# One PSUM pool for a whole attention and feed-forward kernel, with a new prologue order and a new load order

## The chip, the cores and the metric

One core of one Trainium2 chip. The metric is the device time of one execution in microseconds (us), as a median over several runs; the reading is done on a profile of one execution, whose span runs from the first to the last instruction of the program. "PE" is the matrix engine, "PEld" its weight loads, "DVE" VectorE, "ACT" ScalarE, "POOL" GpSimd. PSUM is the memory that PE writes its results to, in banks; a drain is the copy or product with which ScalarE or VectorE empties a bank, and a pair is two banks used as one tile.

## The reference

Eight heads, batch 4, 768 rows of 64. An 8x8 matrix per head is made doubly stochastic by five rounds of exp and normalising, and mixes the eight blocks of 96 rows of keys and of values. Each block of queries then attends to its mixed block. The result, 3072 x 512, goes through a gated feed-forward layer.

```python
k_sorted = einsum('bhij,bhjcd->bhicd', P, k_b); v_sorted = einsum(..., P, v_b)
attn = softmax(scale * q_b @ k_sorted^T);  x = (attn @ v_sorted) -> [B*S, H*D]
g = x @ w_gate;  out = (silu(g) * (x @ w_val)) @ w_out
```

## The kernel before

Work is cut into half batches. Feed-forward block n (there are eight, 0 to 7) takes the x of half batch n: 12 gate and 12 value groups of four matmuls, and output groups of the block before. Attention and mixing of later batches are strewn between them as side work. A "unit" is two heads by four blocks: scores, exp, value product, division, transpose to x. The first half of batch 0 has nothing to hide beside and is the prologue. All loads go through one queue in the order of issue.

```python
wide = tc.tile_pool(name="wide", bufs=1, space=PSUM); psum = wide.__enter__()   # prologue's pool
...
for m in range(0, DF, 256):                 # six pairs of pieces of the gate and value weights
    load_gv(m, m + 256)
load_k(1, 0, C); load_q(1, 0, C); load_v(1, 0, C)      # batch 1
nc.gpsimd.dma_start(out=wo_sb, in_=wo_dram)
...
for n in range(4):                          # batch 0: values and keys in turn
    v_wide(n, "s", slots[2 * n % 3])        # "s": drained by ScalarE
    kq_wide(n, "v", slots[(2 * n + 1) % 3]) # "v": drained by VectorE
...                                         # four units, whole, then:
wide.__exit__(None, None, None)
psum = ctx.enter_context(tc.tile_pool(name="psum", bufs=3, space=PSUM))  # main part
# tags: "att" 3 banks (scores, mixing, x), "av" one pair (value products), "gen" 3 banks
...
def units(b, us):                           # side work, with costs
    ... qk(b, us[n]) / av(b, us[n-1]) / xtr(b, us[n-2], "v")
merge(ffn(0), units(0, range(4, 8)) + kqs(1))
merge(ffn(1), [v_chunk(1, ...) x8] + units(1, range(4)))
```

The softmax here doesn't subtract the row's maximum and nothing guards it: scores larger than these inputs give would overflow.

Of the kernel before, what the change touches and what calls it, by code (L numbers as in the profile page):

```python
# [17 lines left out]
def kernel(  # L18
# [46 lines left out]
    wide = tc.tile_pool(name="wide", bufs=1, space=bass.MemoryType.PSUM)  # L65
    psum = wide.__enter__()
# [67 lines left out]
    for m in range(0, DF, 256):  # L134
        load_gv(m, m + 256)
    load_k(1, 0, C)
    load_q(1, 0, C)
    load_v(1, 0, C)
# [31 lines left out]
    def pair_tile(name, slot):  # L170
        return psum.tile([128, 1024], FP32, name=name, tag=slot)

    def bank_tile(name, slot):
        return psum.tile([128, 512], FP32, name=name, tag=slot)

    p_ps = pair_tile("p_ps", "wa")[0:BH, 0:NB * NB].rearrange("p (i j) -> p i j", j=NB)
# [40 lines left out]
    def kq_chunk(b, cb, eng, tag):  # L217
        nat = kq_tiles[b]
        dst = kqt_tile(b).rearrange("p (n c) -> p n c", c=C)
        rm = rmix[b].rearrange("p two a g i -> p two (a g i)")  # L220
        tp = psum.tile([128, 8, 2 * GI], FP32, name="tkq", tag=tag)
        for lc in range(8):
            for two in range(2):
                nc.tensor.matmul(tp[two * D:(two + 1) * D, lc, :],  # L224
                                 lhsT=nat[:, cb * 8 + lc, :],
                                 rhs=rm[:, two, :], start=True, stop=True)
        drain(eng, dst[:, :, ts(cb, 8)], tp.transpose([0, 2, 1]))

    def v_chunk(b, db, eng, tag):
        rows = highr if b % 2 else lowr  # L230
        dst = vt_tile(b // 2)[:, b % 2]
        mix = vmix[b // 2][rows, b % 2].rearrange("p a b -> p (a b)")
        tp = psum.tile([128, 8, H * NB], FP32, name="tv", tag=tag)
        for ld in range(8):
            at = (db * 8 + ld) * C
            nc.tensor.matmul(tp[:, ld, :], lhsT=vch[rows, at:at + 128], rhs=mix,  # L236
                             start=True, stop=True)
        drain(eng, dst[:, :, ts(db, 8)], tp[0:C].transpose([0, 2, 1]))

    def v_pair_chunk(pair, db, eng, tag):  # L240
        dst = vt_tile(pair).rearrange("p u n e -> p (u n) e")
        mix = vmix[pair].rearrange("p u a b -> p (u a b)")
        tp = psum.tile([128, 4, 2 * H * NB], FP32, name="tv", tag=tag)
        for ld in range(4):
            at = (db * 4 + ld) * C
            nc.tensor.matmul(tp[:, ld, :], lhsT=vch[:, at:at + 128], rhs=mix,  # L246
                             start=True, stop=True)
        drain(eng, dst[:, :, ts(db, 4)], tp[0:C].transpose([0, 2, 1]))
# [4 lines left out]
    def qk(b, u):  # L253
        half, g = divmod(u, H2)
        flat = kqts[b]
        pss = [psum.tile([128, 4, C], FP32, name=f"qk{two}", tag="att") for two in range(2)]
        for i4 in range(4):
            at = (g * NB + half * 4 + i4) * C
            for two in range(2):
                lo = two * D  # L260
                nc.tensor.matmul(pss[two][:, i4, :], lhsT=flat[lo:lo + D, at:at + 128],  # L261
                                 rhs=flat[lo:lo + D, GI * C + at:GI * C + at + C],
                                 start=True, stop=True)
        mine = []
        for two in range(2):
            e = e_all[:, ecount[0] % 8, :]
            ecount[0] += 1
            nc.scalar.activation(e[:, 0:4 * C], pss[two][0:C].rearrange("p a c -> p (a c)"),  # L268
                                 AF.Exp, scale=scale)
            mine.append(e)  # L270
        es[(b, u)] = mine

    def av(b, u, tag="av"):
        half, g = divmod(u, H2)
        vt = vts[b // 2][:, b % 2].rearrange("p (h i) e -> p h i e", h=H)
        av_ps = psum.tile([128, 2, 512], FP32, name="av_ps", tag=tag, bufs=1)
# [14 lines left out]
    def xtr(b, u, eng, tag="att"):  # L291
# [3 lines left out]
        st = sts.pop((b, u))  # L295
        x_ps = psum.tile([128, 4, C], BF16, name="x_ps", tag=tag, bufs=1 if tag == "we" else 3)
        for i4 in range(4):
            nc.tensor.transpose(x_ps[:, i4, :], st[:, i4].rearrange("p a b -> p (a b)"),  # L298
                                ident[0:C, 0:C])
        drain(eng, xts[(b, half)][:, g, :], x_ps.rearrange("p a b -> p (a b)"))  # L300
# [5 lines left out]
    def gate(n, m):  # L306
        xt = xts[divmod(n, 2)]
        if m == 0:
            h_tiles[n] = hpool.tile([128, NFC, TW], BF16, name=f"h{n}", tag="h")
        g_ps = psum.tile([128, TW], FP32, name="g_ps", tag="gen")  # L310
        for kc in range(NKC):
            nc.tensor.matmul(g_ps, lhsT=wg_sb[:, kc, ts(m, 128)], rhs=xt[:, kc, :],  # L312
                             start=(kc == 0), stop=(kc == NKC - 1))
        th_sb = gsp.tile([128, TW], BF16, name="th_sb", tag="th")
# [6 lines left out]
    def value(n, m):  # L321
        xt = xts[divmod(n, 2)]
        v_ps = psum.tile([128, TW], FP32, name="v_ps", tag="gen")
        for kc in range(NKC):
            nc.tensor.matmul(v_ps, lhsT=wv_sb[:, kc, ts(m, 128)], rhs=xt[:, kc, :],  # L325
                             start=(kc == 0), stop=(kc == NKC - 1))
        nc.vector.scalar_tensor_tensor(h_tiles[n][:, m, :], v_ps, 0.5, gs_tiles.pop(m),  # L327
# [4 lines left out]
    def outp(n, t3, part):  # L332
        b, half = divmod(n, 2)
        h_w = h_tiles[n]
        if part == 0:
            o_tiles[n] = psum.tile([128, DM], FP32, name="o_ps", tag="gen")
# [11 lines left out]
    idle_ps = bank_tile("idle_ps", "wd")  # L348

    def fill(n, width=512):  # L350
        for _ in range(n):
            nc.tensor.matmul(idle_ps[:, 0:width], lhsT=warm_sb[:, 0:128], rhs=warm_sb[:, 0:width],
                             start=True, stop=True)

    for _ in range(84):
# [3 lines left out]
                     rhs=v_tiles[0][lowr, HC:HC + 2, :].rearrange("p c d -> p (c d)"),  # L359
                     start=True, stop=True)  # L360
    fill(9)

    w_ps = bank_tile("w_ps", "we").rearrange("p (s i b h) -> p s i b h", s=2, b=B, h=H)

    def weights(half):
        for i in range(NB):
            nc.tensor.matmul(w_ps[half * R:(half + 1) * R, half, i].rearrange("p b h -> p (b h)"),
# [6 lines left out]
    def mix_of(b):  # L374
# [5 lines left out]
            w_ps[lo:lo + R, b % 2, :, b].transpose([0, 2, 1]), op=ALU.mult)  # L380
# [3 lines left out]
            w_ps[0:R, 0, :, b].rearrange("p i (g two) -> p two g i", two=2), op=ALU.mult)  # L384

    def qk_wide(u):
        half, g = divmod(u, H2)
        flat = kqts[0]
        ps = pair_tile("qk", ["wa", "wb", "wc", "wc"][u]).rearrange("p (two n) -> p two n", two=2)
        for i4 in range(4):  # L390
            at = (g * NB + half * 4 + i4) * C
            for two in range(2):
                lo = two * D
                nc.tensor.matmul(ps[:, two, i4 * C:(i4 + 1) * C], lhsT=flat[lo:lo + D, at:at + 128],
                                 rhs=flat[lo:lo + D, GI * C + at:GI * C + at + C],
                                 start=True, stop=True)
        n = ecount[0] % 8
        ecount[0] += 2
        nc.scalar.activation(e_all[:, n:n + 2, 0:4 * C], ps[0:C, :, 0:4 * C], AF.Exp, scale=scale)  # L399
        es[(0, u)] = [e_all[:, n, :], e_all[:, n + 1, :]]  # L400

    mix_of(0)
    kdst = kqt_tile(0).rearrange("p (n c) -> p n c", c=C)
    rm = rmix[0].rearrange("p two a g i -> p two (a g i)")

    def kq_wide(cb, engs, slot):
        tp = pair_tile("tkq", slot).rearrange("p (l n) -> p l n", n=2 * GI)
        for lc in range(16):
            for two in range(2):
                nc.tensor.matmul(tp[two * D:(two + 1) * D, lc, :],  # L410
                                 lhsT=kq_tiles[0][:, cb * 16 + lc, :],
                                 rhs=rm[:, two, :], start=True, stop=True)
        w = 16 // len(engs)
        for n, eng in enumerate(engs):
            drain(eng, kdst[:, :, cb * 16 + n * w:cb * 16 + (n + 1) * w],
                  tp[:, n * w:(n + 1) * w].transpose([0, 2, 1]))

    vdst = vt_tile(0)[:, 0]
    vm = vmix[0][lowr, 0].rearrange("p a b -> p (a b)")

    def v_wide(db, eng, slot):
        tp = pair_tile("tv", slot).rearrange("p (l n) -> p l n", n=H * NB)
        for ld in range(16):
            at = (db * 16 + ld) * C
            nc.tensor.matmul(tp[:, ld, :], lhsT=vch[lowr, at:at + 128], rhs=vm,
                             start=True, stop=True)
        drain(eng, vdst[:, :, ts(db, 16)], tp[0:C].transpose([0, 2, 1]))

    for b in range(1, B):
        mix_of(b)  # L430
    slots = ["wa", "wb", "wc"]
    for n in range(4):
        v_wide(n, "s", slots[2 * n % 3])
        kq_wide(n, "v", slots[(2 * n + 1) % 3])
    kq_wide(4, "s", slots[8 % 3])
    kq_wide(5, "sv", slots[9 % 3])
    fill(3)
    qk_wide(0)
    qk_wide(1)
    qk_wide(2)  # L440
    av(0, 0, "wa")
    av(0, 1, "wb")
    xtr(0, 0, "s", "we")
    av(0, 2, "wa")
    qk_wide(3)
    fill(1)
    xtr(0, 1, "s", "we")
    av(0, 3, "wb")
    fill(1)
    xtr(0, 2, "s", "we")  # L450
    fill(2)
    xtr(0, 3, "s", "we")
    fill(2)
# [3 lines left out]
    wide.__exit__(None, None, None)  # L457
# [102 lines left out]
```

## Time and profile before

| | before |
|---|---|
| time, median of 3 timed runs | 274.19 us (273.6 to 274.84) |
| profiled execution: span, its own time | 273.3 us, 275.36 us |
| PE busy share | 93% |

A block's length is the difference of two starts, that of the first gate matmuls (the prediction lists them).

### The profile page before, as it was taken

Reading aid. Unit: us, or ns where it says so; the run is one execution under the profiler, and the core shown is the slowest. Engines: PE = TensorE matmul, PEld = TensorE weight load, DVE = VectorE, ACT = ScalarE, POOL = GpSimd, SP = SyncE. Lnnn points to the kernel's source line nnn. Section 1 sums busy time; section 2 is a strip of 40 time slices with the busy share of each in tenths; the row PEclk is TensorE's granted clock in tenths of the full one; section 3 lists DMA queues with packets and bytes.
Section 4 is the critical chain, followed back from the end, with each engine's and each line's share of the span. In section 5 each row is a group of like instructions: output and inputs, shape, how many; then the busy total and the mean of one; then the engine's idle time right before and its main releaser. Section 6 shows DMA issues by size and latency. Waiting matters only on the chain.

```text
span 273.3 us, 6511 instructions
## 1 busy us (share of the span) xinstructions
PE 254.0 (93%) x2775; PEld 147.0 (54%) x2775; DVE 163.8 (60%) x362; ACT 125.9 (46%) x242; POOL 47.2 (17%) x46
## 2 busy tenths in 40 slices
PE   3786984999998999999999999999999999999994
PEld 3374452665555556556655556555555555555541
DVE  6685493675369488456359487466566766566500
ACT  3876631446752534439963435335332534323311
POOL 7766300793029300000000000000000000000000
PEclk9998898899999999999999999999999999999998
DMA  6979999909996101101101101101110111011122
GB/s 114 209 98 171 197 224 200 183 4 193 210 232 138 41 1 41 41 2 38 41 0 42 38 0 41 41 4 38 41 38 2 38 38 41 1 41 38 40 77 77
DMA packets 12700, 20.86 MB, mean 76 GB/s; under 512 B 896, under 2 KB 8576, under 8 KB 12032
## 3 DMA queue, kind: packets, MB, share of 16 engines
q0 software_dynamic: 9168, 14.16, 29.4%
q1 hardware_dynamic: 3504, 6.30, 6.2%
q8 instruction: 21, 0.34, 0.5%
q14 instruction: 7, 0.06, 0.1%
HBM read 28.32 MB, written 6.29 MB: 127 GB/s over the span
## 4 chain that ended last, share of the span: by engine, by line
PE 78%; DMA 13%; DVE 3%; POOL 3%; issue 1%; ACT 1%; ACTq 0%; POOLq 0%
PE o_ps L339 23%; PE v_ps L325 22%; PE g_ps L312 21%; DMA kq<-in_q_dram 6%; PE tkq L224 4%; DMA kq<-in_k_dram 4%; DMA wv_sb<-in_moe_w_val_dram 3%; PE qk L261 2%; PE av_ps L281 2%; PE x_ps L298 1%; PE tv L246 1%; PE tv L236 1%; DVE h L327 1%; DVE gs_sb L317 1%; POOL wg_sb L101 1%
## 5 line engine op out<-in xcount | busy, mean ns | idle before, releaser
L317 DVE SCALAR_TENSOR_TENSOR gs_sb<-th_sb,g_ps 128x384 bf16<-128x384 bf16 x96 | 53.0, 552 | 64.0 <-ACT th_sb L315 62.4
L312 PE MATMUL g_ps<-xt,wg_sb 128*128 128x384 bf16 x384 | 78.9, 328 | 0.1
L325 PE MATMUL v_ps<-xt,wv_sb 128*128 128x384 bf16 x384 | 78.9, 328 | 0.0
L315 ACT ACTIVATE th_sb<-g_ps 128x384 bf16<-128x384 f32 x96 | 47.5, 495 | 58.2 <-PE g_ps L312 57.3
L339 PE MATMUL o_ps<-wo_sb,h 128*128 128x512 bf16 x288 | 68.6, 379 | 0.0
L327 DVE SCALAR_TENSOR_TENSOR h<-v_ps,gs_sb 128x384 bf16<-128x384 f32 x96 | 53.3, 555 | 7.8 <-PE v_ps L325 0.6
L312 PEld LDWEIGHTS <-wg_sb 128*128 128x128 bf16 x384 | 34.7, 98 | 22.8 <-issue 1.4
L325 PEld LDWEIGHTS <-wv_sb 128*128 128x128 bf16 x384 | 34.0, 98 | 20.3 <-issue 0.3
L339 PEld LDWEIGHTS <-h 128*128 128x128 bf16 x288 | 26.5, 98 | 27.5
L344 ACT COPY o_sb<-o_ps 128x512 f32<-128x512 f32 x24 | 14.1, 587 | 54.4 <-PE o_ps L339 54.3
L114 POOL COPY vch<-v 64x1536 bf16<-64x1536 bf16 (+1 forms) x10 | 28.0, 2856 | 33.4 <-DMA v<-in_v_dram 33.4
L268 ACT ACTIVATE e_all<-qk 96x384 bf16<-96x384 f32 x56 | 24.3, 488 | 5.7 <-PE qk L261 5.6
L206 ACT CAST vt<-tv 96x512 bf16<-96x512 f32 (+1 forms) x28 | 21.8, 808 | 6.5 <-PE tv L236 3.4
L204 DVE CAST kqt<-tkq 128x512 bf16<-128x512 f32 (+1 forms) x23 | 17.9, 778 | 8.2 <-PE tkq L224 6.4
L287 DVE TENSOR_TENSOR st<-av_ps,r_sb 96x512 bf16<-96x512 f32 x32 | 21.9, 684 | 0.7
L206 ACT CAST kqt<-tkq 128x512 bf16<-128x512 f32 (+1 forms) x20 | 12.1, 604 | 11.4 <-PE tkq L224 10.7
L224 PE MATMUL tkq<-rmix,kq 128*64 128x64 bf16 x576 | 12.9, 200 | 3.6 <-DMA kq<-in_q_dram 3.6
L224 PEld LDWEIGHTS <-kq 128*64 128x64 bf16 x576 | 10.9, 115 | 9.8 <-issue 9.8
L281 PEld LDWEIGHTS <-e_all 96*128 96x128 bf16 x256 | 12.0, 99 | 7.5 <-ACT e_all L399 1.7
L281 PE MATMUL av_ps<-vt,e_all 96*128 96x65 bf16 x256 | 13.7, 195 | 2.0 <-ACT e_all L399 1.2
L298 PEld LDWEIGHTS <-st 96*128 96x128 bf16 x128 | 8.9, 100 | 8.1 <-DVE st L287 3.7
L298 PE MATMUL x_ps<-ident,st 96*128 96x96 bf16 x128 | 11.2, 211 | 2.1 <-DVE st L287 2.1
(59 smaller groups left out, 121.8 us busy)
## 6 DMA issues: line engine op xcount, KB each, us to landing
out_dram<-o_sb SPq DMA_DIRECT2D x24, 256.0 KB, 2.0
kq<-in_q_dram POOLq DMA_DIRECT2D x4, 768.0 KB, 13.2
kq<-in_k_dram POOLq DMA_DIRECT2D x3, 768.0 KB, 13.1
v<-in_v_dram POOLq DMA_DIRECT2D x3, 768.0 KB, 17.7
wg_sb<-in_moe_w_gate_dram POOLq DMA_DIRECT2D x6, 256.0 KB, 9.5
wv_sb<-in_moe_w_val_dram POOLq DMA_DIRECT2D x6, 256.0 KB, 10.0
wo_sb<-in_moe_w_out_dram POOLq DMA_DIRECT2D x1, 1536.0 KB, 24.2
v<-in_v_dram POOLq DMA_DIRECT2D x2, 384.0 KB, 5.6
```

Of the source, the lines that this page charges most:

```text
L114: eng.tensor_copy(dst, src.transpose([0, 2, 1]))
L206: nc.scalar.copy(dst, src)
L224: nc.tensor.matmul(tp[two * D:(two + 1) * D, lc, :], lhsT=nat[:, cb * 8 + lc, :], rhs=rm[:, two, :], start=True, stop=True)
L268: nc.scalar.activation(e[:, 0:4 * C], pss[two][0:C].rearrange("p a c -> p (a c)"), AF.Exp, scale=scale)
L281: nc.tensor.matmul(o[:, two, i4, :], lhsT=e[:, i4 * C:i4 * C + 128], rhs=vt[:, 2 * g + two, half * 4 + i4, :], start=True, stop=True)
L298: nc.tensor.transpose(x_ps[:, i4, :], st[:, i4].rearrange("p a b -> p (a b)"), ident[0:C, 0:C])
L312: nc.tensor.matmul(g_ps, lhsT=wg_sb[:, kc, ts(m, 128)], rhs=xt[:, kc, :], start=(kc == 0), stop=(kc == NKC - 1))
L315: nc.scalar.activation(th_sb, g_ps, AF.Tanh, scale=0.5)
L317: nc.vector.scalar_tensor_tensor(gs_sb, th_sb, 1.0, g_ps, op0=ALU.add, op1=ALU.mult)
L325: nc.tensor.matmul(v_ps, lhsT=wv_sb[:, kc, ts(m, 128)], rhs=xt[:, kc, :], start=(kc == 0), stop=(kc == NKC - 1))
L327: nc.vector.scalar_tensor_tensor(h_tiles[n][:, m, :], v_ps, 0.5, gs_tiles.pop(m), op0=ALU.mult, op1=ALU.mult)
L339: nc.tensor.matmul(o_ps, lhsT=h_w[:, m, ts(t3, 128)], rhs=wo_sb[:, m, :], start=(m == 0), stop=(m == NFC - 1))
```

## The change

Its intent: keep one PSUM pool from start to end (pairs "a" and "b", one bank "x", three banks "gen"), so that no pool is swapped; share the drains of the prologue between two engines and mix all values of batch 0 before the keys; load batch 1's keys and queries before the last pair of weight pieces; place side work by fractions of a block; start the first gate and value matmuls on those head pairs whose x is there.

```diff
-    wide = tc.tile_pool(name="wide", bufs=1, space=bass.MemoryType.PSUM)
-    psum = wide.__enter__()
+    psum = ctx.enter_context(tc.tile_pool(name="psum", bufs=1, space=bass.MemoryType.PSUM))
-    for m in range(0, DF, 256):
+    for m in range(0, 1280, 256):
         load_gv(m, m + 256)
     load_k(1, 0, C)
     load_q(1, 0, C)
+    load_gv(1280, DF)
...
-    def qk(b, u):                            # two single banks, two exps
+    def qk(b, u, tag="b"):                   # one pair, one exp over both
-    def av(b, u, tag="av"):
+    def av(b, u, tag="a"):
...                                           # x of the main part: tag "att" -> the one bank "x"
+    v_chunk(0, 0, 8, "v", "gen"); v_chunk(0, 8, 16, "s", "a"); ...   # all values
+    kq_chunk(0, 0, 16, "v", "a"); kq_chunk(0, 16, 16, "s", "b"); ... # then keys
...
+    early(0, (0,)); early(1, (0,))           # first gate and value on head pair 0
+    x3 = ...                                 # x of the fourth unit
+    early(0, (1, 2)); early(1, (1, 2)); early(2, (0, 1, 2))
+    for n in range(3): early(n, (3,))
...
-    merge(ffn(1), [v_chunk x8] + units(1, range(4)))
+    merge(ffn(1), spread([v_chunk x4 of double size], 0.4, 0.6) + spread(units(1, range(4)), 0.6, 0.97))
-    merge(ffn(2), units(1, range(4, 8)) + kqs(2))
+    merge(ffn(2), spread(units(1, range(4, 8)), 0.0, 0.45) + spread(kqs(2), 0.45, 0.95))
```

(Cut: more warm-up fillers, the copy of the mixing weights to SBUF, the same spreading of the later blocks.)

## The prediction

> **What bounds the kernel now.** I read the page first for the busiest engine, then the chain that ended last, then the chain and the waits inside the first 60 us, then a table by stage.
>
> ```profile
> PE 254.0 (93%) x2775; PEld 147.0 (54%) x2775; DVE 163.8 (60%) x362; ACT 125.9 (46%) x242; POOL 47.2 (17%) x46
> PEclk9998898899999999999999999999999999999998
> PE 78%; DMA 13%; DVE 3%; POOL 3%; issue 1%; ACT 1%; ACTq 0%; POOLq 0%
> ```
>
> The matrix engine carries the chain for 78%, but 13% of it is DMA. The chain between 10 and 52 us shows where that part lies:
>
> ```profile
> 4.98 10.80 DMA kq<-in_k_dram
> ...
> 19.67 9.42 DMA wv_sb<-in_moe_w_val_dram
> 29.09 0.29 issue
> 29.38 15.68 DMA kq<-in_q_dram
> 45.06 0.14 issue
> 45.19 0.69 PE tkq L224 x32
> 45.89 1.00 PE v_ps L325 x4
> 46.89 1.28 PE g_ps L312 x4
> ```
>
> Until 45.19 us nothing that PE does is on the chain. Batch 0's keys land, then the weights (twelve pieces), then batch 1's keys and queries, and only then can PE mix batch 1. The waits of PE from 29.6 to 52 us, and the stages, say what it costs (columns of the table: stretch, length, busy time of PE, PEld, DVE, ACT and POOL, clock, DMA share, GB/s):
>
> ```profile
> PE tkq L224 <- DMA kq<-in_q_dram: 3.6, 1, 3.6
> 12.20:21.80 9.60, 7.72 (x278) 6.49 (x278) 7.04 (x13) 6.03 (x7) 5.97 (x9) 1.00 0.81 114
> 21.80:29.64 7.84, 6.13 (x87) 3.77 (x87) 3.74 (x11) 4.82 (x8) 3.91 (x7) 0.78 1.43 189
> 29.64:41.50 11.86, 10.80 (x124) 6.41 (x124) 9.37 (x22) 5.67 (x13) 1.84 (x3) 1.00 1.27 216
> 41.50:50.00 8.50, 4.94 (x77) 2.94 (x77) 3.06 (x6) 2.15 (x4) 0.60 (x1) 0.80 1.07 197
> 59.45:90.54 31.09, 30.38 (x278) 16.62 (x277) 18.16 (x38) 15.11 (x31) 14.78 (x11) 1.00 0.79 170
> 90.54:121.79 31.25, 31.18 (x405) 18.14 (x404) 21.26 (x42) 13.97 (x29) 0.66 (x1) 1.00 0.08 27
> ```
>
> The cuts are the starts of the feed-forward blocks (48 gate matmuls each): 29.64, 59.45, 90.54, 121.79, 152.92, 184.17, 210.97, 237.77. From 59 us on PE is full, and a block there only gets shorter by matmuls or switches that vanish. The loose time is before 59 us: 9.6 us of mixing for batch 0, 7.8 us for its first four attention units, and 8.5 us with a 3.6 us wait and a clock of 0.80.
>
> **What the Trainium skill says.** "TensorE: Matmul & The Clock Gate", Part 1, has PE drop to half clock after about one idle window of 3.4 us. The trace agrees: after the 3.6 us wait, the clock record shows 0.5 from 46.26 for 3.41 us, and four matmuls take 1.00 and 1.28 us against 0.65 elsewhere. "DMA: Bandwidth & Descriptors", Queues, rings and completion order: each DMA engine consumes its descriptors in ring order. Here the pool's loads landed in the order of issue, so moving one load moves those behind it by its length. "VectorE: DVE Perf Modes", Why PSUM operands drop a tier: an fp32 PSUM source runs at 1x. The trace agrees: 0.69 us for 128x512 and 1.22 for 128x1024, so one drain in place of two saves only 0.16. "PSUM — Partial Sum Buffer", Specifications: eight banks of 2 KiB per partition. Both pools fill them: before, 3+3+2 in the main part; after, two pairs (a, b), one bank for x and three "gen" banks.
>
> **The change part by part.**
>
> *Load order.* The sixth pair of weight pieces goes behind batch 1's keys and queries. In the trace the tenth weight piece landed at 34.45, the eleventh and twelfth at 35.76 and 37.6, keys at 41.22, queries at 45.06. Keys then take 3.62 us and queries 3.84, so without the pair the queries land at 34.45+3.62+3.84 = 41.9. That is 3.15 us earlier. The late pair lands near 44.9 and is first wanted by the gate of chunk 10, three matmul groups after batch 1's mixing begins, near 46. Values of batch 1 (49.3) and the output weights (56.2) keep their times, since the same bytes precede them.
>
> *Batch 0's mixing.* Now it starts at 13.09 and the last drain ends at 21.73. VectorE works 5.01 us on four wide key drains, 0.69 on the last, and 1.3 on mixes of batches 1 to 3 in between. ScalarE has four value drains of 1.06, one of 1.01 and one of 0.59. After, the drains are shared: VectorE 0.67+1.2+0.67 for values and 1.22+0.69+1.22+0.69 for keys, 6.4 us; ScalarE 1.06+0.6+0.6 and 1.01+0.59+0.59+1.01, 5.5 us, plus a 0.4 us copy of the weights. The mixes of the other batches read that copy and stand behind the drains, where VectorE waited 1.77 us anyway. The filler and warm-up in front end before the softmax does (11.5), so weights start at about 11.7, not 12.21, values at 12.55. 12.95 + 6.4 + about 0.6 of hand-overs gives the first score matmul at T = 20.0, where it is 21.79.
>
> *First four units.* Counted from T with before's durations (exp 0.81 for a pair or 2 x 0.49, reciprocal 0.20, multiply 0.69): the four results are ready at 2.6, 3.5, 4.7, 5.8. Two units' x leave in one ScalarE copy (estimate 0.8, ends 5.2), the third at 5.7, the fourth by VectorE at 6.5. Nine of the twelve first gate and value matmuls run on the pairs present, and only three wait for the last: all twelve end at T+7.7 = 27.7. Before, the first gate starts at 29.64, T+7.85, and three groups need 1.96 us more, to 31.6. The price: the three groups hold all three "gen" banks, so the next value waits until ScalarE's tanh (0.49) and VectorE's product (0.55) free one, about T+8.6 = 28.6. Net 3.0 us ahead.
>
> *Block 0.* Fourteen groups of 0.652 and the four units of the second half (3.2 us of PE: 0.37 score, 0.265 value, 0.17 transpose each) come before batch 1's mixing: 28.6+9.1+3.2 = 40.9. VectorE must do 14 products of 0.55, 0.35 of copies and four units of 1.23, 12.9 us in the 12.3, so PE is held about 0.5 more: 41.4. The queries come at 41.9. The 3.56 us wait shrinks to some 0.5 us, and the half-clock stretch (3.4 us of work took 5.0, 1.6 lost) should vanish. The rest is 7 groups and six chunks of 0.72: 4.6+4.3 = 8.9, plus 0.3 for drains of 1.22 at tight spacing. Block 1 starts at 51.2, where it is 59.45: 8.2 us. Of these, about 3 are the prologue, 1.6 the clock, the rest the wait.
>
> *Later blocks.* The matmul counts are unchanged (768 mixing, 192 value mixing, 256+256+128 attention, 768+288 feed-forward). The eight half-row value chunks of batch 1 become four; each run costs about 0.19 more for its switches (first matmul to step 0.258 where 0.163 is usual, last 0.122 against 0.03), 0.75 saved. The spread by fractions puts two whole groups between the last unit's value matmul and its transpose, where 0.9 us was lost at 86 us and 0.6+0.3 near 148: I count 0.5 and 0.7 back. Blocks 2 and 4 gain 0.15 each; 5, 6 and the tail are as before.
>
> Sum: 51.2 + 29.8 + 31.1 + 30.4 + 31.1 + 26.8 + 26.8 + 35.6 = 262.8 of span. The timed median is 0.9 above the profiled span (274.19 against 273.3): 263.7. I add 0.6 for waits I have not seen: 264.3.
>
> **Rivals.** *The next transfer takes over.* With block 1 at 51.2 the output weights (56.2) are wanted at 51.2+8 x 0.652 = 56.4, and batch 1's values, rearranged by POOL until about 60.6, at about 61.0. For: neither transfer moves. Against: both are met by a few tenths. If the margins fail it costs 0.5 to 2 us: 265 to 266. *VectorE becomes the bound of block 0.* It has 22.4 us of work for PE's 21.2 there. For: 9.37 busy of 11.86 already. Against: the second stretch, with drains split, is lighter. It would add 1 to 2 us: 265 to 266. *The clock falls in the prologue.* It was 0.78 in the second stretch. For: PE waits for exp and multiply there as before; a 3.4 us window at half clock under the twelve matmuls costs up to 1.7 us. Against: seven fillers of 0.22 fill the gaps. 265.5. *All is hidden:* if the queries still landed at 45, only the clock and the later blocks would gain, 270; the ring order speaks against it.
>
> **Range and chances.** The three costly rivals together reach 268, and nothing found makes it slower; the best case without the 0.6 and with the whole of the lost waits back is 262. So 264.3, 262.0 to 267.8. Two per cent is 268.7: faster 0.93, within 0.06, slower 0.01.
>
> **What would show it.** Right: batch 1's queries landing at about 42 and a wait under 1 us there, no half clock after it, first score matmul near 20.0, block 1 starting near 51. Wrong: the queries landing after 44, a new wait of more than 1 us on the output weights or on the rearranged values, a gap of more than 1.5 us on the "gen" banks after the first twelve matmuls, or blocks 1 to 4 longer than before.

## The result, and the profile after

The changed kernel took 270.81 us (269.81 to 271.1, four runs) against 274.19. Ratio 0.987, 95% interval 0.9834 to 0.9905; a ratio is the mean time of one kernel's fast runs over that of the other's fast runs of the same rounds, so not quite the ratio of the medians. It is faster by 1.3%, where 3.6% was forecast. It lies outside the range, and within the two per cent to which the prediction gave a chance of 0.06.

The page of the changed kernel, first busy times and the clock:

```profile
span 267.7 us, 6445 instructions
PE 250.7 (94%) x2756; PEld 146.5 (55%) x2781; DVE 169.9 (63%) x362; ACT 114.9 (43%) x189; POOL 47.3 (18%) x46
PEclk9999999999999999999999999999999999999999
PE 82%; DVE 9%; ACT 5%; issue 3%; ACTq 0%; DVEq 0%
```

The clock is full in all slices, and DMA has gone from the chain that ended last (it was 13%). In its place stand VectorE with 9% and ScalarE with 5%: the chain now passes through drains and exps. The stages by block follow, cut at block starts (columns as in the prediction: stretch, length, busy times of PE, PEld, DVE, ACT and POOL, clock, DMA share, GB/s). Before, blocks 3 and 4:

```profile
121.79:152.92 31.13, 30.54 (x278) 18.50 (x277) 17.36 (x36) 20.92 (x39) 0.00 (x0) 1.00 0.07 27
152.92:184.17 31.25, 31.18 (x405) 18.14 (x404) 21.27 (x42) 13.97 (x29) 0.00 (x0) 1.00 0.07 27
```

After, the prologue's mixing and units, and blocks 0 to 4 (the first row of the fence is the prologue):

```profile
12.20:25.28 13.08, 11.77 (x344) 8.92 (x347) 10.67 (x23) 9.57 (x16) 7.94 (x12) 1.00 0.94 134
25.28:51.92 26.64, 24.34 (x375) 14.75 (x373) 21.11 (x43) 11.68 (x20) 7.59 (x8) 1.00 1.23 207
51.92:81.73 29.81, 29.52 (x274) 16.80 (x276) 20.14 (x39) 12.58 (x21) 13.48 (x11) 1.00 0.81 169
81.73:113.98 32.25, 31.10 (x402) 18.18 (x404) 20.36 (x39) 13.53 (x22) 8.29 (x3) 1.00 0.17 46
113.98:146.22 32.24, 30.52 (x275) 18.72 (x277) 21.55 (x40) 15.16 (x23) 0.00 (x0) 1.00 0.07 25
146.22:178.47 32.25, 31.10 (x402) 18.18 (x404) 20.35 (x39) 13.53 (x22) 0.00 (x0) 1.00 0.07 26
```

Blocks 2, 3 and 4 have the same matmuls as before, and in blocks 2 and 4 the same PE busy time within 0.1 us, yet each is 1.0 to 1.1 us longer than before: PE has gaps there. The two kernels' accounts, in us:

| | before | after | change | forecast |
|---|---|---|---|---|
| start of block 1 | 59.45 | 51.92 | -7.53 | 51.2 |
| block 1 | 31.09 | 29.81 | -1.28 | 29.8 |
| block 2 | 31.25 | 32.25 | +1.00 | 31.1 |
| block 3 | 31.13 | 32.24 | +1.11 | 30.4 |
| block 4 | 31.25 | 32.25 | +1.00 | 31.1 |
| blocks 5 and 6 | 53.6 | 53.3 | -0.3 | 53.6 |
| rest | 35.5 | 35.9 | +0.4 | 35.6 |
| span | 273.3 | 267.7 | -5.6 | 262.8 |

The waits of PE between 80 and 180 us name the gaps (columns: engine and line, what it waited for, us in total, times, longest). Before:

```profile
PE x_ps L298 <- DVE st L287: 1.2, 2, 0.7
```

After:

```profile
PE x_ps L304 <- DVE xt L204: 2.1, 3, 0.8
PE g_ps L323 <- DVE h L346: 0.8, 1, 0.8
PE qk L267 <- ACT e_all L276: 0.7, 3, 0.2
```

All three are new. Before, a transpose waited for its own input (st, the divided result). Now it waits for xt, the copy that empties the bank of the transpose before it. A gate waits for h, the product that empties a "gen" bank. And scores wait for an exp, that is for the pair "b" to be read. The timeline of the changed kernel at one such place (start, length, engine, line, operation, and in brackets the idle time and its releaser; lines of other instructions left out where dots stand):

```profile
93.89 0.35 PEld L304 LDWEIGHTS <-st 96*128 96x128 bf16 x4
94.05 0.34 PE L304 MATMUL x_ps<-ident,st 96*128 96x96 bf16 x4
...
94.22 0.82 PE L323 MATMUL g_ps<-xt,wg_sb 128*128 128x384 bf16 x4
94.34 0.68 DVE L293 TENSOR_TENSOR st<-av_ps,r_sb 96x512 bf16<-96x512 f32 x1
94.94 0.54 DVE L346 SCALAR_TENSOR_TENSOR h<-v_ps,gs_sb 128x384 bf16<-128x384 f32 x1
...
95.40 0.34 DVE L204 COPY xt<-x_ps 128x384 bf16<-128x384 bf16 x1
95.80 0.33 PE L304 MATMUL x_ps<-ident,st 96*128 96x96 bf16 x4 [0.76 <-DVE xt L204]
```

The third unit's transpose is done at 94.39. Its copy has to queue behind the fourth unit's multiply (94.34) and a product (94.94), and starts at 95.40. The fourth transpose had its input from 95.02 on, but there is one bank "x", so PE stands until 95.80. Before, x took its bank from the three of the tag "att". Between the two transposes stands one gate group (94.22).

The listing counts idle time from the modelled ends of matmuls. By their starts PE lost more: from the last gate matmul to the transpose it is 1.08 us, where 0.16 is the usual step, so 0.92. The losses of single waits named below (0.92, 0.71, 0.94, 0.31, 0.28, 0.89) are by starts.

### The profile page after: what moved, and what is told of

It is laid out like the page before. It is cut to its first block, busy times and chain, and to the rows that moved or that the text cites. A ratio compares the mean times of both kernels' runs of the same rounds, so it can differ in the third digit from the quotient of the medians.

```text
span 267.7 us, 6445 instructions
## 1 busy us (share of the span) xinstructions
PE 250.7 (94%) x2756; PEld 146.5 (55%) x2781; DVE 169.9 (63%) x362; ACT 114.9 (43%) x189; POOL 47.3 (18%) x46
## 3 DMA queue, kind: packets, MB, share of 16 engines
q0 software_dynamic: 9168, 14.16, 29.8%
## 4 chain that ended last, share of the span: by engine, by line
PE 82%; DVE 9%; ACT 5%; issue 3%; ACTq 0%; DVEq 0%
PE o_ps L358 23%; PE v_ps L341 21%; PE g_ps L323 21%; PE tkq L226 6%; PE qk L267 3%; PE av_ps L287 2%; PE x_ps L304 2%; DVE h L346 2%; ACT e_all L276 2%; PE tv L238 2%; DVE gs_sb L333 2%; ACT th_sb L331 1%; DVE st L293 1%; PE tv L248 1%; DVE vt L204 1%
## 5 line engine op out<-in xcount | busy, mean ns | idle before, releaser
L341 PE MATMUL v_ps<-xt,wv_sb 128*128 128x384 bf16 x380 | 77.6, 326 | 0.8 <-DVE gs_sb L333 0.8
L323 PE MATMUL g_ps<-xt,wg_sb 128*128 128x384 bf16 x376 | 76.6, 326 | 0.8 <-DVE h L346 0.8
L331 ACT ACTIVATE th_sb<-g_ps 128x384 bf16<-128x384 f32 x96 | 46.9, 490 | 67.8 <-PE g_ps L323 65.2
L358 PE MATMUL o_ps<-wo_sb,h 128*128 128x512 bf16 x268 | 67.3, 380 | 1.3 <-DVE h L346 0.2
L276 ACT ACTIVATE e_all<-qk 96x768 bf16<-96x768 f32 x30 | 24.0, 802 | 13.5 <-PE qk L267 13.3
L291 DVE RECIPROCAL r_sb<-av_ps 96x8 f32<-96x8 f32 x32 | 6.4, 200 | 19.3 <-PE av_ps L287 19.2
L226 PEld LDWEIGHTS <-kq 128*64 128x64 bf16 x768 | 14.1, 112 | 7.1 <-issue 7.0
L204 DVE CAST kqt<-tkq 128x1024 bf16<-128x1024 f32 (+1 forms) x13 | 14.8, 1138 | 4.5 <-PE tkq L226 4.5
L226 PE MATMUL tkq<-rmix,kq 128*64 128x64 bf16 x768 | 16.6, 197 | 0.8 <-issue 0.8
L206 ACT CAST kqt<-tkq 128x1024 bf16<-128x1024 f32 (+1 forms) x13 | 12.1, 948 | 8.4 <-PE tkq L226 8.3
```

Source lines behind the costliest of these rows:

```text
L226: nc.tensor.matmul(tp[two * D:(two + 1) * D, lc, :], lhsT=kq_tiles[b][:, at + lc, :], rhs=rm[:, two, :], start=True, stop=True)
L276: nc.scalar.activation(e_all[:, n:n + 2, 0:4 * C], wide[0:C, :, 0:4 * C], AF.Exp, scale=scale)
L323: nc.tensor.matmul(g_ps, lhsT=wg_sb[:, kc, ts(m, 128)], rhs=xt[:, kc, :], start=(kc == 0), stop=(kc == NKC - 1))
L331: nc.scalar.activation(th_sb, g_ps, AF.Tanh, scale=0.5)
L341: nc.tensor.matmul(v_ps, lhsT=wv_sb[:, kc, ts(m, 128)], rhs=xt[:, kc, :], start=(kc == 0), stop=(kc == NKC - 1))
L358: nc.tensor.matmul(o_ps, lhsT=h_w[:, m, ts(t3, 128)], rhs=wo_sb[:, m, :], start=(m == 0), stop=(m == NFC - 1))
```

## The experiments

Nine kernels start from the changed one (the control is the changed kernel itself), three from the kernel before. All twelve gave the right result. Ratios are against the kernel before, run on the same chip in the same rounds; three chips were used, one for each group of four.

| run | median us | ratio (95% interval) | span | block 1 starts | blocks 1, 2, 3, 4 |
|---|---|---|---|---|---|
| after_again | 270.55 | 0.9863 (0.982 to 0.9906) | 267.3 | 51.54 | 29.82, 32.25, 32.23, 32.25 |
| load_only | 276.0 | 1.0056 (1.0018 to 1.0094) | 272.9 | 57.05 | 33.07, 31.25, 31.12, 31.26 |
| old_load | 272.51 | 0.9921 (0.9888 to 0.9954) | 271.6 | 55.82 | 29.81, 32.25, 32.23, 32.26 |
| no_early | 269.77 | 0.9825 (0.9796 to 0.9853) | 267.0 | 51.28 | 29.81, 32.25, 32.23, 32.25 |
| x_scalar | 267.65 | 0.9759 (0.9716 to 0.9801) | 267.8 | 54.55 | 29.72, 31.59, 31.53, 31.59 |
| x_gen | 269.89 | 0.9833 (0.981 to 0.9857) | 268.6 | 53.27 | 29.77, 31.89, 31.53, 31.89 |
| qk_swap | 268.66 | 0.9796 (0.9772 to 0.982) | 266.6 | 51.75 | 29.82, 31.94, 31.93, 31.94 |
| combo | 265.89 | 0.9696 (0.9655 to 0.9738) | 263.3 | 51.89 | 29.73, 31.28, 30.28, 31.28 |
| load_warm | 276.2 | 1.0019 (0.9981 to 1.0058) | 273.8 | 55.01 | 36.01, 31.26, 31.12, 31.26 |
| load_warm_vlate | 272.94 | 0.9927 (0.9895 to 0.9958) | 269.8 | 55.65 | 30.97, 31.26, 31.12, 31.26 |
| old_banks | 267.38 | 0.9709 (0.9679 to 0.9739) | 265.3 | 53.53 | 30.25, 31.23, 30.21, 31.23 |
| combo_whole | 264.81 | 0.9647 (0.9604 to 0.969) | 261.9 | 50.5 | 29.72, 31.28, 30.28, 31.28 |

A profile is of one run, and the first 60 us vary: after, x_scalar, x_gen, qk_swap and combo differ before block 1 only in the four units of block 0, and block 1 starts anywhere from 51.75 to 54.55. Blocks 2 to 4 repeat within 0.02 us in the two profiles of the changed kernel. So the blocks are compared by the profile and the whole by the ratio.

### Control: after_again

No edit.

> Control: the changed kernel once more on the chip of the other three runs. Both theories: 270 to 271.5, span 267.5 to 269, blocks 2, 3 and 4 about 32.2 each. It also tells how far one profiled span lies below or above the timed median (the prediction took 0.9; the records of both kernels suggest about 2).

It came as expected, with six runs from 269.42 to 272.84. The profiled run's own time is 269.42, 2.1 above its span of 267.3. In the first pair of profiles it is the same: 275.36 against 273.3 and 269.81 against 267.7.

### What the load order does: old_load, load_only

old_load: the changed kernel, weights first again.

```diff
-    for m in range(0, 1280, 256):
+    for m in range(0, DF, 256):
         load_gv(m, m + 256)
     load_k(1, 0, C)
     load_q(1, 0, C)
-    load_gv(1280, DF)
```

> The changed kernel with all weights ahead of batch 1's keys, as before. My theory: queries land near 44.6, where PE asks for them at 42.6, so 2 us more than the changed kernel, 272.5 to 273, and perhaps a short half clock on top. Rival (the later place of batch 1's mixing already covers the load): within 0.5 us of the changed kernel.

Median 272.51, as expected: 0.6% more than the changed kernel on the same chip. The queries landed at 45.62 and PE waited for them (waits of PE from 26 to 70 us, old_load):

```profile
PE tkq L225 <- DMA kq<-in_q_dram: 2.9, 1, 2.9
```

After it the clock record shows half speed from 45.29 for 3.41 us, and block 1 starts at 55.82 instead of 51.54. So the load order is a real part of the gain, about 2 us by the medians (the two intervals overlap a little, but the wait is in the trace), and the new prologue does not cover the late load. The profiled run is the slowest of its six, at 273.72, so the 4.3 us at block 1 overstate it.

load_only: the kernel before with the load order of the changed one.

```diff
-    for m in range(0, DF, 256):
+    for m in range(0, 1280, 256):
         load_gv(m, m + 256)
     load_k(1, 0, C)
     load_q(1, 0, C)
+    load_gv(1280, DF)
```

> The kernel before with the new load order alone. My theory (the wait for batch 1's queries and the half clock after it cost 5.2 us in the kernel before, and the blocks 2 to 4 of the changed kernel give 3 us of the gain back): queries land near 41.9, the 3.6 us wait falls under 0.7, no half clock after it, 4 to 5 us faster than before, so as fast as the whole change or up to 1 us faster (269 to 270.5). Rival (the wait was hidden by VectorE's backlog and comes back elsewhere): under 2 us faster, 272 or more.

This was a miss: 276.0 us, 0.6% slower than before, where I had expected 4 to 5 us less. The queries did land at 41.88, the wait for them is gone, and block 0 takes 24.82 us instead of 29.81, 5.0 less, as my theory said. The stages of load_only show where it went (prologue mixing, prologue units, block 0, block 1):

```profile
12.20:23.72 11.52, 10.09 (x278) 8.69 (x277) 7.07 (x13) 6.23 (x7) 7.23 (x11) 0.70 0.84 122
23.72:32.23 8.51, 7.31 (x86) 4.41 (x87) 3.83 (x11) 4.93 (x8) 3.94 (x7) 0.62 1.45 196
32.23:57.05 24.82, 23.77 (x368) 14.66 (x369) 19.16 (x40) 11.92 (x26) 8.47 (x4) 0.99 1.04 186
57.05:90.12 33.07, 30.44 (x278) 16.62 (x276) 18.15 (x38) 15.12 (x31) 17.60 (x12) 1.00 0.75 160
```

In the prologue PE ran at a clock of 0.70 and 0.62, so block 0 began at 32.23, 2.6 us later than in the profile of before. In the kernel before such a delay is hidden, because PE waits for the queries until 45 us anyway. Its runs on that chip agree: the five with a mean clock of 0.978 to 0.981 have a mean span of 272.6, the five with 0.993 or 0.994 one of 272.7. And block 1 is 2.0 us longer: its first value chunk waits for the values of batch 1, which POOL rearranges until about 60 us. 5.0 - 2.6 - 2.0 leaves 0.4, the difference of the two spans (273.3 and 272.9). This is the account of one pair of profiles: load_only's is the fastest of its six runs, before's a slow one. By the medians load_only is 1.2 us slower, not 0.4 faster, and these 1.6 us are not accounted for.

### The two things that ate it: load_warm, load_warm_vlate

load_warm: load_only with the changed kernel's warm-up.

```diff
-    for _ in range(84):
+    for _ in range(82):
-                     rhs=v_tiles[0][lowr, HC:HC + 2, :]
+                     rhs=v_tiles[0][lowr, 0:2, :]
-    fill(9)
+    fill(11)
```

> load_only with the changed kernel's warm-up in front (82 small matmuls, the first half of the values as marker, eleven fillers). Theory: load_only lost in the prologue what it won at the queries, because PE ran at half clock from 15.5 to 22.4 and 25.8 to 32.6 us and block 0 began at 32.2, and nothing hid it any more. With PE warm from about 11 us on, block 0 begins at 29.7 or before, and the time falls 2 to 3.5 us against load_only (273 to 274). Rival (the half clock comes from the idle times of the prologue itself, not from its start): half clock stays in the record and the time stays at 275 to 276.

The expected gain did not come; the time is 276.2. The half clock did not go: it stands in the record from 15.54 for 6.83 us, though not from 25.8 to 32.6 as in load_only, and block 0 starts at 30.34. So the warm-up in front is not what keeps PE at full clock. What PE saved there it lost at once in a longer wait (waits of PE from 26 to 70 us, and a piece of the chain that ended last: start, length, what):

```profile
PE tv L237 <- POOL vch L114: 3.3, 1, 3.3
```

```profile
30.25 18.18 DMA v<-in_v_dram
...
51.38 8.38 POOL vch L114 x3
59.75 0.05 issue
59.80 0.54 PE tv L237 x8
60.34 1.40 PE g_ps L313 x4
```

The next transfer, batch 1's values with their rearrangement on POOL, has taken the place of the queries. It ends at 59.8, and at 60.5 in load_only, where block 1 began 2 us later; and the matmuls behind it run at half clock again (1.40 us for four). The prediction had this rival, but for the changed kernel, whose value chunks come later; the kernel before asks for them first thing in block 1.

load_warm_vlate: the same, with the value chunks of batch 1 moved behind the first output group of block 1.

```diff
-    merge(ffn(1), [(0.28, lambda db=db: v_chunk(1, db, "s", "att")) for db in range(8)]
+    merge(ffn(1), [(1.5, lambda: None)] + [(0.28, lambda db=db: v_chunk(1, db, "s", "att")) for db in range(8)]
           + units(1, range(4)))
```

> load_warm with the value chunks of batch 1 put after the first output group of block 1. Theory: in load_only they waited 2.0 us for the values that POOL rearranges until 60 us (rival of the prediction, met by the changed kernel's place at 0.4 of block 1). The wait vanishes, 1 to 2 us less than load_warm, about 271 to 272: load order, warm start and late values together give what the whole change gives. Rival: the two microseconds come back as another wait in block 1, same time as load_warm.

272.94 us, 3.3 less than load_warm, more than expected, and 0.7% less than before; but not the 271 to 272 named, so the three together do not give what the whole change gives. Block 1 is back to 30.97 and no wait for POOL remains. So here the load order is worth something only together with a later place of the values. (The later place was not run with the old load order; in the kernel before no wait for POOL was listed that it could remove.) Up to block 0, what still separates this kernel from the changed one is the prologue: block 0 starts at 30.98, and its mixing chunks take 1.07 us where the warm ones take 0.69 (until 22.4 us, when its clock record begins).

In all four profiles with the old prologue (before, load_only, load_warm, load_warm_vlate) some stretch before 33 us runs at half clock; in the ten others, with the new prologue, none does up to the first feed-forward matmul. The old prologue went with low clocks, then, but the runs do not separate which part of the new one does it, the shared drains or the fillers between chunks.

### Does running the first groups per head pair help: no_early

(Lines joined and shortened.)

```diff
-    early(0, (0,)); early(1, (0,))
     x3 = xt_tile("x", 1); x_to(x3[:, 0], 0, 3); drain("v", ...)
-    early(0, (1, 2)); early(1, (1, 2)); early(2, (0, 1, 2))
-    for n in range(3): early(n, (3,))
-    gate_out(0, 0, first[0]); value_out(0, 0, first[1]); gate_out(0, 1, first[2])
+    early(0, range(NKC)); gate_out(0, 0, first[0])
+    early(1, range(NKC)); value_out(0, 0, first[1])
+    early(2, range(NKC)); gate_out(0, 1, first[2])
```

> The changed kernel, but the first gate, value and gate run whole after the fourth unit's x, not per head pair. My theory: the three early groups hold all three banks until tanh and product free one (a wait of 0.84 us at 28.7), so running them early gains only 0 to 0.3 us: 270.6 to 271.2. Rival (the early matmuls are a real gain, as predicted, of about 1 us): 271.5 to 272.

269.77 against 270.55, and block 1 starts at 51.28 against 51.54: no gain from the early matmuls, rather a small loss (the intervals overlap). In the changed kernel the next value group starts at 28.73, after a wait for a bank:

```profile
28.73 0.81 PE L341 MATMUL v_ps<-xt,wv_sb 128*128 128x384 bf16 x4 [0.84 <-DVE gs_sb L333]
```

In no_early it starts at 28.30, with the twelve matmuls run whole just before:

```profile
26.19 0.94 PE L457 MATMUL g_ps<-xt,wg_sb 128*128 128x384 bf16 x4
26.97 0.81 PE L457 MATMUL v_ps<-xt,wv_sb 128*128 128x384 bf16 x4
27.61 0.81 PE L457 MATMUL g_ps<-xt,wg_sb 128*128 128x384 bf16 x4
28.30 0.81 PE L341 MATMUL v_ps<-xt,wv_sb 128*128 128x384 bf16 x4
```

Three groups finished together hold all three "gen" banks until tanh and product have run. One group finished first lets its drain start while the second and third compute: the first tanh starts at 27.16 in no_early and at 27.60 in the changed kernel.

### Banks or schedule: old_banks, x_gen, x_scalar, qk_swap

old_banks: the changed kernel, but a pool swap after the first part, and the main part in three "att" banks, one "av" pair and three "gen" banks, on the new fractions. (Shortened.)

```diff
-    psum = ctx.enter_context(tc.tile_pool(name="psum", bufs=1, ...))
+    first_pool = tc.tile_pool(name="first", bufs=1, ...); psum = first_pool.__enter__()
...
+    first_pool.__exit__(None, None, None)
+    psum = ctx.enter_context(tc.tile_pool(name="psum", bufs=3, ...))
...   # scores, mixing chunks (8 or 4 wide) and x take "att", value products "av"
```

> The changed kernel with the main part in the banks of before (three single att banks for scores, keys, values and x, one pair for value products, three gen), on the new schedule by fractions; first part untouched. Theory A (the single bank of x and the pair b made blocks 2 to 4 longer): the waits of x for the drain of the unit before and the 0.3 us waits of the second scores vanish; blocks 2, 3, 4 at 31.2, 30.6, 31.2 instead of 32.25, 32.23, 32.26; block 1 0.7 longer by the eight value chunks; 1.5 to 2.5 us faster than the changed kernel, 268 to 269. Rival B (the schedule by fractions made them longer, not the banks): blocks 2 to 4 stay at 32 or above.

267.38 us, ratio 0.9709: better than expected. Blocks 2 to 4 are 31.23, 30.21 and 31.23, so 1.0, 2.0 and 1.0 us shorter than in the changed kernel, on the same fractions, and no wait of PE over the listing's limit is left between 80 and 180 us:

```profile
115.01:145.22 30.21, 30.21 (x278) 18.57 (x277) 17.36 (x36) 21.17 (x39) 0.00 (x0) 1.00 0.07 27
```

PE is busy for all 30.21 us of block 3. So the schedule by fractions is a gain (it takes 0.9 us off block 3 of the kernel before, 31.12), and the change of banks, with the wider drains that go with it, undoes it. This stands although the wait for a bank at 27.7 us is 2.0 us in this profile with its pool swap (0.84 in the changed kernel), with a half clock from 30.18 for 3.41 us after it.

x_gen: only the bank, for the last unit of each four.

```diff
-    def xtr(b, u):
+    def xtr(b, u, tag="x"):
-        x_ps = xt_tile("x", 1)[:, 0]
+        x_ps = xt_tile(tag, 1)[:, 0]
-                todo.append(lambda u=us[n - 2]: drain("v", *xtr(b, u)))
+                todo.append(lambda u=us[n - 2]: drain("v", *xtr(b, u, "gen" if u == us[-1] else "x")))
```

> The changed kernel with only the last unit of each four transposed into a gen bank; drains stay on VectorE. Theory A (bank count): x no longer waits for the drain of the unit before, only for its own multiply: the waits shrink by 0.5 to 0.7 each, 1.5 to 2.5 us off, 268.5 to 269.3, unless the gen bank is missed by gate and value, then a wait of up to 0.5 shows at them. Theory B (multiply): 0 to 0.5 off.

269.89, less of a gain than the expected 268.5 to 269.3. The wait of x for xt is gone and blocks 2 to 4 are 0.36, 0.71 and 0.36 shorter. But gate and value miss the bank: a wait of 0.28 shows behind x in blocks 2 and 4, and blocks 5 and 6, which had no wait, become 27.15 instead of 26.64. 1.4 us won, 1.0 lost. A second bank for x takes the wait away, but one of the three "gen" banks is missed elsewhere.

x_scalar: only the drain's engine.

```diff
-                todo.append(lambda u=us[n - 2]: drain("v", *xtr(b, u)))
+                todo.append(lambda u=us[n - 2]: drain("s", *xtr(b, u)))
```

> The changed kernel with x of the main part drained by ScalarE in place of VectorE; still one bank for x. Theory A (the one bank of x is held by a drain that stands behind the fourth unit's multiply and a product in VectorE's queue): the four waits of x (0.89, 0.92, 0.71, 0.92) shrink to 0.2 to 0.3 each, some 2.4 us off, and VectorE gets 28 x 0.35 = 10 us lighter, which may take part of the 0.94 near 129 us: 268 to 268.6. Theory B (the waits are for the multiply itself, the bank only comes last): under 1 us off. Theory C (PE is the bound and the blocks grew by something else): no change.

267.65 us, ratio 0.9759. Blocks 2 to 4 are 0.66, 0.70 and 0.66 shorter and blocks 5 and 6 unchanged: the bank is enough if it is emptied at once. The gain is that of theory A, for the three waits there. The waits of PE from 80 to 180 us have lost the line of x and kept the other two:

```profile
PE g_ps L323 <- DVE h L346: 0.8, 1, 0.8
PE qk L267 <- ACT e_all L276: 0.7, 3, 0.2
```

qk_swap: the first scores of each four units in pair "b", the others in "a", all value products in "b".

```diff
-                todo.append(lambda u=us[n]: qk(b, u))
+                todo.append(lambda u=us[n]: qk(b, u, "b" if u == us[0] else "a"))
-                todo.append(lambda u=us[n - 1]: av(b, u))
+                todo.append(lambda u=us[n - 1]: av(b, u, "b"))
```

> The changed kernel with the scores of the first unit of each four in pair b and of the others in pair a, and all value products in pair b, so that the second scores do not follow the first in one pair. Theory A: the waits of 0.3 us of the second scores in blocks 0, 2, 3, 4 (and 0.15 in block 1) vanish, 1.2 to 1.4 us off, 269.4 to 269.7. Rival (the pair taken by the value products clashes instead): no gain or 0.5 worse.

268.66, ratio 0.9796. Blocks 2 to 4 are each 0.31 shorter, which is the wait of the second scores for the first exp; the listing of waits has lost that line. Over the whole it did a little better than the 1.2 to 1.4 us expected.

### Together: combo, combo_whole

combo is x_scalar and qk_swap, and the eight value chunks of batches 2 and 3 drained by ScalarE alone:

```diff
-    spread([lambda n=n: v_pair_chunk(1, n * 8, 8, "sv"[n % 2], "ba"[n % 2]) for n in range(8)], 0.0, 0.5)
+    spread([lambda n=n: v_pair_chunk(1, n * 8, 8, "s", "ba"[n % 2]) for n in range(8)], 0.0, 0.5)
```

> x_scalar and qk_swap together, and the eight value chunks of batches 2 and 3 drained by ScalarE alone (VectorE's 1.22 us drains stood ahead of a product that gate waited 0.77 us for at 130 us). Theory A: 2.4 + 1.3 + 0.8 off, blocks 2 to 4 at 31.0, 30.3, 31.0, so 266 to 266.8: faster than both. If ScalarE becomes the bound in block 3 (eight drains of 1.1 beside tanh), a wait for it appears there of up to 1 us.

265.89 us, ratio 0.9696, below both kernels. The stages of blocks 2 to 4 of combo:

```profile
81.62:112.90 31.28, 31.20 (x405) 18.01 (x404) 19.34 (x35) 15.08 (x26) 9.40 (x4) 1.00 0.20 52
112.90:143.18 30.28, 30.28 (x277) 18.62 (x276) 16.43 (x32) 21.17 (x31) 0.00 (x0) 1.00 0.07 27
143.18:174.46 31.28, 31.20 (x405) 18.00 (x404) 19.34 (x35) 15.07 (x26) 0.00 (x0) 1.00 0.07 27
```

Three small edits in the one pool, all about who empties a bank and when, take 1.0, 2.0 and 1.0 us off these blocks. The third edit was not run alone: after the 0.70 of x_scalar and the 0.31 of qk_swap, 0.95 of the 2.0 in block 3 are left for it. ScalarE is busy 21.17 of 30.28 us in block 3 and no wait for it appears.

combo_whole is combo with the first groups whole, as in no_early (the same edit).

> The best so far (x and late values drained by ScalarE, scores and value products in changed pairs) without the per-pair first matmuls. If running the first gate and value per head pair gives nothing because the three banks are held, this is 0.5 us faster to equal, 265.2 to 266; if it is a gain that the slower runs hid, 0.5 to 1 slower.

264.81 us, ratio 0.9647, 3.5% faster than before; its best run took 263.73. It is the fastest version. Against combo (another chip, overlapping intervals) the difference of 0.5% is not settled.

## Why the prediction was wrong, point by point

- **Load order: right.** The queries landed at 41.49 (forecast 41.9), the late weight pair at 45.3 (44.9), the output weights at 55.59 (56.2), and no half clock followed. The sentence on ring order that the prediction cites from the Trainium skill ("DMA: Bandwidth & Descriptors") stands in a paragraph on the queues of SyncE and ScalarE, which adds that completion need not keep the order. That the loads of POOL's queue landed in order is shown by the traces, all fourteen. old_load shows the part it has. That the earlier load alone would expose the values is shown by load_only and load_warm; the changed kernel asks for them at 61.8 us, after POOL was done with them at 59.45 (the copies began at 48.16 and took 11.29).
- **Prologue: right.** First score matmul at 20.11 (20.0), twelve matmuls done near 27.7 (27.7), the next group after the wait for a bank at 28.73 (28.6).
- **First matmuls per head pair: right in its wait, wrong in what was left out.** The net gain of 3.0 us counted the early matmuls as part of it. no_early shows that they add nothing, so the start came as forecast although one of its causes was wrong.
- **Block 0: nearly right.** Block 1 began at 51.92 against 51.2. PE was held by VectorE's queue more than by the queries: a transpose lost 0.89 us at 41 us, again for the one bank "x".
- **Later blocks: this step failed.** Its terms 31.1, 30.4 and 31.1 hold no wait for a bank. The prediction said: "The spread by fractions puts two whole groups between the last unit's value matmul and its transpose ... I count 0.5 and 0.7 back. Blocks 2 and 4 gain 0.15 each". Two groups do stand between value product and transpose. The prediction listed the banks ("one bank for x"), but I had not looked at the one group between the third and the fourth transpose, which now share one bank, nor at the one group between the first and the second scores, which share pair "b". The waits are 0.92 and 0.31 us in blocks 2 and 4, and 0.71, 0.31 and 0.94 in block 3, the last for a product behind a 1.22 us drain of values on VectorE. Blocks 2 to 4 came out 1.15, 1.84 and 1.15 longer than forecast, 4.1 us of the 4.9 by which the span was missed. The order of PE's instructions and the bank counts were known; the time of a bank's release through VectorE's queue was not worked out. combo, in which the three causes are removed, has blocks 2 to 4 at 31.28, 30.28 and 31.28, against a forecast of 31.1, 30.4 and 31.1: the forecast was of a kernel without these waits. Block 1 came out at 29.81 for 29.8, in part by luck: 0.75 had been counted for wider value chunks, and old_banks, with eight narrow ones, is only 0.44 longer there (its banks differ too), so the spread seems to have given more than its 0.5.
- **From span to time: mis-sized.** I added 0.9, the median of before less the span of its profile. But that profiled run was a slow one: its own time was 275.36, 2.06 above its span. The changed kernel's profiled run is 2.1 above its span as well, and was the fastest of its four. In no run on record is this difference under 1.97. With the 0.6 of allowance, 1.5 had been set where 3.1 came. This is the other 1.6 us of the miss of 6.5.
- **The rivals.** The next transfer did not hold the changed kernel up in its profile. VectorE did, though not as the bound of block 0, but as the engine that frees banks in blocks 2 to 4. "Blocks 1 to 4 longer than before" stood among the signs of a wrong forecast, and for blocks 2 to 4 it came true.

What stays open: why the same kernel varies by 1 to 5 us between fast runs. Part of it is the landing of loads (the queries landed at 41.49 and 42.27 in two profiles of the changed kernel, at 43.6 in that of x_scalar, where PE waited for them again). Another part is a wait without a releaser in the middle of the fourth mixing chunk of batch 1, before its 13th matmul, in six of the ten profiles with the new prologue: 0.26 us in the changed kernel, 1.78 in x_scalar:

```profile
50.69 0.51 PE L226 MATMUL tkq<-rmix,kq 128*64 128x64 bf16 x20 [1.78 <-issue]
```

The traces point to the loading of instructions, which no run tests. Each has transfers of 16 KB on the queue that the page of the profile calls "q8 instruction", and one of them ends just before: in the six profiles with the wait the 13th matmul starts 1.27 to 1.48 us after that end, in the four without it 1.54 to 1.68. In the changed kernel the transfer ended at 46.62, in x_scalar at 49.21.

## What to carry to other kernels

When banks are merged into fewer, wider tiles, list for each tile the two successive uses that stand closest on PE, and compare that distance with the way of its release: the drain's own time plus all that stands before it in that engine's queue. An early transfer is worth only what the next one in the queue leaves of it, so move the demand for the next one too. And check a profile's span against that same run's time before carrying a sum of spans over to a median.

## What the Trainium skill lacked or had wrong

- "TensorE: Matmul & The Clock Gate", Part 1: its table has the clock drop after an idle window of about 3.4 us. Here less idleness was enough: the 3.41 us before a drop had PE busy for 1.44 us in old_banks, 1.93 in load_only and 2.25 in the kernel before. The page also tells of drops after short idles, but not how much work keeps the clock. Busy time alone, as the profile gives it, does not tell either: in the kernel before the stretch just ahead of that had 2.21, one of load_warm 2.06, and no drop followed.
- "TensorE: Matmul & The Clock Gate", Part 3: it gives about 4 ns from tile to tile, but not the price of changing the tile shape; "TensorEngine Tiling (Array Packing)" says that a change of mode drains the engine, without a time. In the changed kernel a gate or value group's last matmul before a run of 64 rows or 64 columns (scores, mixing of keys and queries, half-row mixing of values) takes 0.255 to 0.259 us to the next start instead of 0.163, and the last of such a run 0.122 to 0.135.
- "PSUM — Partial Sum Buffer", Summary: "Evacuate promptly" has no measure of what lateness costs. A copy of 0.34 us that began 1.0 us after the transpose it empties held PE for 0.76 us.
- No page that I read has a wait of PE without a releaser inside a run of like matmuls. Here it was 0.2 to 1.8 us at the same matmul in six profiles, ending 1.27 to 1.48 us after a 16 KB transfer of instructions.
